# Sinkhorn attention and a bilinear feed-forward: k mixes of two head pairs together, v mixes in their own slots, and the last output tile copied by two engines

## The chip, the cores and the metric

The kernel runs on one core of a Trainium2 chip. The time is device microseconds of one execution; the metric is the median over runs. The kernel before has a median of 260.51 us of 3 runs (257.8 to 262.68).

## The reference

Four batches, eight heads, 768 positions, head size 64, and for every head an 8 x 8 matrix `sort_net`. Five rounds of exponential and row and column normalisation (Sinkhorn) turn it into P. P then mixes the eight blocks of 96 positions of k and of v, each block of q attends to its own mixed block, and the result goes through a bilinear feed-forward.

```python
for _ in range(5):
    P = np.exp(P - np.max(P, axis=-1, keepdims=True))
    P = P / (np.sum(P, axis=-1, keepdims=True) + 1e-09)
    P = P / (np.sum(P, axis=-2, keepdims=True) + 1e-09)
k_sorted = einsum('bhij,bhjcd->bhicd', P, k_blocks)     # v_sorted likewise
scores = q_block @ k_sorted_block.T / sqrt(64)          # 96 x 96 per block
attn_out = softmax(scores) @ v_sorted_block
x = attn_out with heads side by side                    # 3072 x 512
out = ((x @ w_a) * (x @ w_b)) @ w_out                   # 512 -> 1536 -> 512
```

## The kernel before, in words

Work is cut into 16 *pairs* g of two heads; pair g belongs to batch b = g // 4, and hp = g % 4. A pair's attention has these stages:

- `stage_q` (L165) transposes q on TensorE (PE) into a PSUM tile `q_ps`, and VectorE (DVE) copies it to `qT`. For pairs of batches 2 and 3, `q_by_dma` (L191) does this with one DMA transpose on SP's queue instead.
- `stage_mix` (L180) mixes k or v with P: 12 matmuls of 128 columns, each with a weight of 64 columns, so that the two heads of a pair use the left and the right half of the array. The result is a PSUM tile `mix` of two banks. `evac_k` or `evac_k_natural` (L212) copies it to `kT` on ScalarE (ACT).
- `stage_v_natural` (L196), for batches 2 and 3: two matmuls of 384 columns with full weights (L201), a DVE copy to `vn`, a store `vd` to DRAM on SP's queue (L207), and a load `vs` from there on POOL's queue (L208). For earlier batches v is mixed as k is, and `stage_v` (L239) transposes it on PE.
- `stage_scores` (L224): 8 matmuls into a PSUM tile `sc` and an exponential on ACT; once per half of the blocks.
- `stage_o` (L249): 8 matmuls of the exponentials with `vs` into `o_ps`, then a reciprocal and a product on DVE into `xp`; once per half.
- `to_xT` (L277, on PE and DVE) or `to_xT_dma` (L288, SP's queue) transposes `xp` into the feed-forward's input `xT`.

The feed-forward of a batch has 72 *steps*. 48 of them are `ffn_a` and `ffn_b` (L307, L314): four matmuls of 384 columns at L302 into a PSUM bank `pf`. After `ffn_a`, ACT copies it to `a_sb`; after `ffn_b`, DVE multiplies the two into `hT`. The last 24 steps are `ffn_out` (L328): three matmuls of 512 columns at L335 into `po`. Every fourth of these ends a tile of 128 rows, which ACT (c even) or DVE (c odd) copies to `o_sb` (L340), and two stores on SP's queue take it to `out`.

The order on PE is written by hand throughout. The order on ACT and DVE is by hand only in the parts of the program under `manual_schedule(engines=fast)`: the lead, and the block just ahead of the steps (L479 to L486). Elsewhere a scheduler orders ACT, DVE, SP and POOL by when things come ready in its own reckoning, and each of them then runs strictly in that order.

The lead (up to about 38 us in the profile) does Sinkhorn, the loads of weights, and the first halves of pairs 0 to 3. Then the loop of steps begins, and attention is hung between the steps: `after[s]` lists what follows step s. The dictionary `second` (L488) places the second halves of pairs 0 to 3: Q1 is `stage_q` for blocks 4 to 7, S1 the scores, V1 the transpose of v, O1 the product with v, X1 the transpose into `xT`. For later pairs, `C` (L451) mixes, `R` (L468) does the scores and `O` (L474) the rest. For batches 2 and 3 their slots are R at r = (b-1) 72 + 8 + 15 hp, C at r - 12 and O at r + 6.

PSUM has a pool `psA` of two tiles of two banks (mix, sc, o_ps), `psB` of one tile (q_ps, vs_ps, xt_ps) and `psF` of three banks (pf, po). The pool `ld` holds three each of k, v and q; `load_pair(g + 3)` (L81, POOL's queue) is called in `C(g)`, and its transfers wait until pair g has been read. `kT` has 5 buffers, `vs` 3.

Of the kernel before, what the change touches and what calls it, by code (L numbers as in the profile page):

```python
# [22 lines left out]
def kernel(  # L23
# [11 lines left out]
    nc = tc.nc  # L35
    P = 128
    B, H, S, D = q.shape
# [3 lines left out]
    DMODEL = H * D  # L41
# [5 lines left out]
    HP = H // 2  # L47
# [31 lines left out]
    BD = 2  # L79
# [76 lines left out]
    def copy(eng, out, in_):  # L156
        if eng is nc.scalar:
            nc.scalar.copy(out=out, in_=in_)  # L158
        else:
            eng.tensor_copy(out=out, in_=in_)  # L160

    def blocks(h):
        return (0, NB) if h is None else (h * NBH, NBH)

    def stage_q(g, pool, tag, eng, h=None):  # L165
        q2 = loaded[g][2]
        i0, n = blocks(h)
        p0, np_ = i0 * CG, n * CG
        q_ps = pool.tile([P, NCH, np_], BF16, tag=tag, name="q_ps")
        for c in range(NCH):  # L170
            for e in range(2):
                nc.tensor.matmul(q_ps[e * D:(e + 1) * D, c, :],  # L172
                                 lhsT=q2[p0:p0 + np_, e, c * D:(c + 1) * D],
                                 rhs=ident[p0:p0 + np_, p0:p0 + np_], is_transpose=True)
        if (g, "qT") not in st:
            st[g, "qT"] = qtp.tile([P, NB, NCH, CG], BF16, tag="qT", name="qT")
        copy(eng, st[g, "qT"][:, i0:i0 + n].rearrange("p i c t -> p c i t"),
             q_ps.rearrange("p c (i t) -> p c i t", i=n))

    def stage_mix(g, what, pool, tag):  # L180
        src2 = loaded[g][0 if what == "k" else 1]
        mix = pool.tile([P, 2, 512], FP32, tag=tag, name="mix")
        for c in range(NCH):
            for e in range(2):
                nc.tensor.matmul(  # L185
                    mix[e * D:(e + 1) * D, c // 4, c % 4 * P:(c % 4 + 1) * P],
                    lhsT=src2[:, e, c * D:(c + 1) * D],
                    rhs=s_all[:, 2 * g + e], start=True, stop=True)
        st[g, what] = mix

    def q_by_dma(g):  # L191
        qT = qtp.tile([P, NCH, P], BF16, tag="qT", name="qT")
        nc.sync.dma_start_transpose(out=qT, in_=loaded[g][2].rearrange("p e w -> p (e w)"))
        st[g, "qT"] = qT
# [17 lines left out]
    def evac_k_natural(g, eng):  # L212
        copy(eng, _ap(kTs[g % NKV], 0, [[S + PAD, P], [NCH, P], [1, NCH]]),
             _ap(st[g, "k"], 0, [[1024, P], [1, P], [P, NCH]]))

    def evac_k(g, eng):
        copy(eng, _ap(kTs[g % NKV], 0, [[S + PAD, P], [CG, NCH], [BLK, NB], [1, CG]]),
             _ap(st[g, "k"], 0, [[1024, P], [P, NCH], [CG, NB], [1, CG]]))

    def evac_v(g, eng, h):  # L220
        copy(eng, _ap(vTs[g % NKV], h * HK, [[2 * HK, P], [CG, NCH], [BLK, NBH], [1, CG]]),
             _ap(st[g, "v"], h * NBH * CG, [[1024, P], [P, NCH], [CG, NBH], [1, CG]]))
# [105 lines left out]
    def ffn_out(b, t, c, part, pool):  # L328
        hT = hTs[b]
        c0 = t * HW + c * P  # L330
        if part == 0:
            st[b, t, c] = pool.tile([P, DMODEL], FP32, tag="F", name="po")
        po = st[b, t, c]
        for m in range(part * KO // NPO, (part + 1) * KO // NPO):
            nc.tensor.matmul(po, lhsT=hT[:, m, c0:c0 + P], rhs=w_out_sb[:, m, :],  # L335
                             start=(m == 0), stop=(m == KO - 1))
        if part < NPO - 1:
            return
        o_sb = ffp.tile([P, DMODEL], FP32, tag="o_sb", name="o_sb", bufs=6)
        copy(nc.scalar if c % 2 == 0 else nc.vector, o_sb, po)  # L340
        for u in range(2):
            nc.sync.dma_start(
                out=_ap(out, (b * S + t * NBH * BLK + 2 * c + u) * DMODEL,
                        [[NCH * DMODEL, NBH * CG], [1, DMODEL]]),
                in_=o_sb[u * NBH * CG:(u + 1) * NBH * CG])
# [18 lines left out]
    with tc.manual_schedule(engines={mybir.EngineType.PE}):  # L364
# [68 lines left out]
        with tc.tile_pool(name="psA", bufs=2, space=PSUM) as psA, \  # L433
                tc.tile_pool(name="psB", bufs=1, space=PSUM) as psB, \
                tc.tile_pool(name="psF", bufs=3, space=PSUM) as psF:
            def Q1(g):
                stage_q(g, psB, "B", nc.vector, 1)

            def S1(g):
                stage_scores(g, psA, "A", 1)  # L440

            def V1(g):
                stage_v(g, psB, "B", 1)

            def O1(g):
                stage_o(g, psA, "A", 1)

            def X1(g):
                to_xT(g, psB, "B", 1, nc.vector)

            def C(g):  # L451
                if g >= BD * HP:
                    stage_mix(g, "k", psA, "A")
                    evac_k_natural(g, nc.scalar)
                    stage_v_natural(g, psA, "A", nc.vector)
                else:
                    stage_q(g, psB, "B", nc.vector)
                    stage_mix(g, "k", psA, "A")
                    evac_k(g, nc.scalar)
                    stage_mix(g, "v", psA, "A")  # L460
                    for h in range(2):
                        evac_v(g, nc.vector, h)
                if g + 3 < B * HP:
                    load_pair(g + 3)
                if BD * HP <= g + 1 < B * HP:
                    q_by_dma(g + 1)

            def R(g):  # L468
                stage_scores(g, psA, "A", 0)
                stage_scores(g, psA, "A", 1)  # L470
                if g < BD * HP:
                    stage_v(g, psB, "B")

            def O(g):  # L474
                stage_o(g, psA, "A", 0)
                stage_o(g, psA, "A", 1)
                to_xT_dma(g)

            with tc.manual_schedule(engines=fast):  # L479
                g = HP - 1  # L480
                parts = {}
                for n_, (m, w_sb) in enumerate(((0, w_a_sb), (0, w_b_sb), (1, w_a_sb))):
                    parts[m, w_sb is w_b_sb] = ffn_mm(0, m, 0, w_sb, psF, 0, KA - 1)
                    if n_ == 0:
                        stage_o(g, psA, "A", 0)
                to_xT(g, psB, "B", 0, nc.vector)  # L486

            second = {0: [(Q1, 0)], 1: [(Q1, 1)], 2: [(S1, 0)], 3: [(V1, 0)], 4: [(S1, 1)],  # L488
                      5: [(O1, 0), (V1, 1)], 6: [(Q1, 2)], 7: [(X1, 0)], 8: [(S1, 2), (O1, 1)],
                      9: [(V1, 2)], 10: [(Q1, 3)], 11: [(X1, 1)], 12: [(S1, 3), (O1, 2)],  # L490
                      13: [(V1, 3)], 14: [(X1, 2)], 15: [(O1, 3)], 17: [(X1, 3)]}

            NSL = 4 * KO + 2 * 3 * NPO
            after = {s: [] for s in range(-NSL, B * NSL)}
            for s, u in second.items():
                after[s] += u
            for g in range(HP, B * HP):
                b, hp = divmod(g, HP)
                if b < BD:
                    r = (b - 1) * NSL + 28 + 10 * hp  # L500
                    c_, o_ = r - 4, r + 4
                else:
                    r = (b - 1) * NSL + 8 + 15 * hp
                    c_, o_ = r - 12, r + 6
                after[c_].append((C, g))
                after[r].append((R, g))
                after[o_].append((O, g))
            s = 0
            for b in range(B):
                steps = []  # L510
                for m, t in ([(m, t) for t in range(2) for m in range(KO)] if b == 0 else
                             [(m, t) for m in range(KO) for t in range(2)]):
                    for f, u in ((ffn_a, False), (ffn_b, True)):
                        pf = parts.pop((m, u), None) if (b, t) == (0, 0) else None
                        steps.append(lambda f=f, m=m, t=t, b=b, pf=pf: f(b, m, t, psF, pf))
                for t in range(2):
                    for c in range(3):
                        for part in range(NPO):
                            steps.append(lambda t=t, c=c, part=part, b=b:
                                         ffn_out(b, t, c, part, psF))  # L520
                for step in steps:
                    step()
                    for f, g in after[s]:
                        f(g)
                    s += 1
# [29 lines left out]
```

## Time and profile before

| what | value |
|---|---|
| median of the timed runs | 260.51 us |
| the profiled execution's own time | 626.5 us |
| its span | 624.7 us |
| first pf matmul, last matmul's end | 38.54 us, 620.08 us |
| PE weight loads, busy | 249.5 us (40%) |
| chain that ended last, PE's share | 96% |
| stores of out, 48 of 128 KB | 2.3 us to land |
| vd store; vs load (192 KB), to land | 3.9 us; 3.9 to 4.0 us (medians) |

The profiled execution was far slower than the timed ones. In the page, a group is a line of code, engine, operation and tiles, with the number of instructions, busy time, mean length, and the idle time ahead of them with what ended it. In the chain of waits in order of time, each row has a start, a length, an engine, a tile and a line. In the timeline, the bracket at the end of a row gives the engine's idle time before it and what ended it.

### The profile page before, as it was taken

How to read it: one execution, taken by the hardware profiler on the slowest of the kernel's cores; microseconds unless marked ns; L12 is line 12 of the kernel's file. 1: busy time of each engine (PE TensorE's matmuls, PEld its weight loads, DVE VectorE, ACT ScalarE, POOL GpSimd, SP SyncE). 2: the span in 40 equal slices, each digit the busy share in tenths (PEclk: the TensorE clock that was granted, in tenths of full speed). 3: DMA queues.
4: the chain of work that ended last, by engine and by line, in shares of the span. 5: the costliest groups of instructions: out<-in, count | busy, mean ns of one | idle time of the engine just before them, and what ended most of it. 6: DMA issues, size and time to landing. Idle time of an engine off the chain costs nothing.

```text
span 624.7 us, 5272 instructions
## 1 busy us (share of the span) xinstructions
PE 612.4 (98%) x2140; PEld 249.5 (40%) x2153; DVE 120.7 (19%) x268; ACT 99.2 (16%) x176; POOL 62.3 (10%) x83
## 2 busy tenths in 40 slices
PE   9999999999999999999999999999999999999997
PEld 2554445544443344444333344444433334334221
DVE  4342322322211122121110122121201111111000
ACT  2322112122010121212010121212010011111000
POOL 5561001101230010101000100000000000000000
DMA  9796002314493151312122301010112100000021
GB/s 152 112 202 105 1 0 39 41 10 51 74 128 72 42 64 26 50 26 50 43 47 47 67 1 38 9 31 14 26 34 47 34 0 0 1 0 0 18 50 34
DMA packets 50776, 27.88 MB, mean 45 GB/s; under 512 B 30400, under 2 KB 47296, under 8 KB 50752
## 3 DMA queue, kind: packets, MB, share of 16 engines
q0 software_dynamic: 29712, 15.73, 19.2%
q1 hardware_dynamic: 21040, 11.81, 8.4%
q8 instruction: 17, 0.28, 0.2%
q14 instruction: 7, 0.06, 0.0%
HBM read 29.89 MB, written 7.86 MB: 60 GB/s over the span
## 4 chain that ended last, share of the span: by engine, by line
PE 96%; DMA 2%; issue 1%; POOL 1%; DVE 0%; ACT 0%
PE pf L302 55%; PE po L335 27%; PE o_ps L258 3%; PE w_ps L361 3%; PE mix L185 2%; PE sc L230 2%; DMA w_b_sb<-in_moe_w_b_dram 2%; PE q_ps L172 1%; PE mix L201 1%; PE vs_ps L244 1%; PE xt_ps L283 0%; POOL w_a_sb L143 0%; POOL w_b_sb L143 0%; POOL s_all L351 0%; ACT o_sb L158 0%
## 5 line engine op out<-in xcount | busy, mean ns | idle before, releaser
L302 PE MATMUL pf<-xT,w_a_sb 128*128 128x384 bf16 x384 | 194.0, 684 | 1.0 <-DMA w_b_sb<-in_moe_w_b_dram 0.5
L302 PE MATMUL pf<-xT,w_b_sb 128*128 128x384 bf16 x384 | 192.2, 681 | 0.0
L335 PE MATMUL po<-w_out_sb,hT 128*128 128x512 bf16 x276 | 168.5, 832 | 3.7 <-issue 3.7
L319 DVE TENSOR_TENSOR hT<-a_sb,pf 128x384 bf16<-128x384 bf16 x96 | 53.2, 555 | 270.8 <-PE pf L302 270.7
L302 PEld LDWEIGHTS <-w_a_sb 128*128 128x128 bf16 x384 | 65.6, 173 | 98.0 <-issue 96.7
L302 PEld LDWEIGHTS <-w_b_sb 128*128 128x128 bf16 x384 | 64.3, 172 | 91.5 <-issue 90.8
L335 PEld LDWEIGHTS <-hT 128*128 128x128 bf16 x288 | 49.2, 173 | 112.0 <-issue 111.8
L311 ACT CAST a_sb<-pf 128x384 bf16<-128x384 f32 x96 | 46.0, 479 | 301.5 <-PE pf L302 301.5
L158 ACT COPY o_sb<-po 128x512 f32<-128x512 f32 x16 | 9.4, 586 | 134.1 <-PE po L335 114.7
L160 DVE COPY o_sb<-po 128x512 f32<-128x512 f32 x8 | 5.5, 692 | 98.1 <-PE po L335 98.1
L264 DVE TENSOR_TENSOR xp<-o_ps,rec 96x512 bf16<-96x512 f32 x32 | 21.7, 682 | 0.7
L361 PE MATMUL w_ps<-warm_sb 128*128 128x512 bf16 x32 | 19.3, 819 | 1.7 <-DVE warm_sb L71 1.2
L262 DVE RECIPROCAL rec<-o_ps 96x8 f32<-96x8 f32 x32 | 6.4, 201 | 50.8 <-PE o_ps L258 50.8
L160 DVE CAST vn<-mix 128x768 bf16<-128x768 f32 x8 | 7.7, 957 | 16.4 <-PE mix L201 16.4
L236 ACT ACTIVATE eT_113<-sc 96x768 bf16<-96x768 f32 x12 | 9.2, 804 | 8.8 <-PE sc L230 8.7
L258 PEld LDWEIGHTS <-eT_113 96*128 96x128 bf16 x96 | 8.9, 149 | 4.3 <-issue 3.7
L258 PE MATMUL o_ps<-vs_116,eT_113 96*128 96x65 bf16 x96 | 9.3, 284 | 0.3 <-issue 0.3
L361 PEld LDWEIGHTS <-warm_sb 128*128 128x128 bf16 x33 | 4.8, 157 | 11.6 <-issue 10.3
L236 ACT ACTIVATE eT_114<-sc 96x768 bf16<-96x768 f32 x10 | 7.6, 803 | 9.6 <-PE sc L230 9.5
L351 POOL TENSOR_TENSOR s_all<-mask,p_col 128x1024 bf16<-128x1024 bf16 (+1 forms) x5 | 7.2, 1455 | 12.5 <-ACT p_col L403 12.5
L236 ACT ACTIVATE eT_115<-sc 96x768 bf16<-96x768 f32 x10 | 7.6, 803 | 3.4 <-PE sc L230 3.4
L258 PEld LDWEIGHTS <-eT_114 96*128 96x128 bf16 x80 | 6.8, 143 | 2.9 <-issue 2.9
(202 smaller groups left out, 244.7 us busy)
## 6 DMA issues: line engine op xcount, KB each, us to landing
out_dram<-o_sb SPq DMA_DIRECT2D x48, 128.0 KB, 2.3
w_a_sb<-in_moe_w_a_dram POOLq DMA_DIRECT2D x4, 384.0 KB, 7.7
w_b_sb<-in_moe_w_b_dram POOLq DMA_DIRECT2D x4, 384.0 KB, 9.0
w_out_sb<-in_moe_w_out_dram POOLq DMA_DIRECT2D x3, 512.0 KB, 8.8
vd<-vn SPq DMA_DIRECT2D x8, 192.0 KB, 3.9
q_first<-in_q_dram POOLq DMA_DIRECT2D x2, 384.0 KB, 8.1
vs_118<-vd POOLq DMA_DIRECT2D x3, 192.0 KB, 4.0
vs_116<-vd POOLq DMA_DIRECT2D x3, 192.0 KB, 3.9
```

What stands on the lines that cost most here:

```text
L158: nc.scalar.copy(out=out, in_=in_)
L160: eng.tensor_copy(out=out, in_=in_)
L185: nc.tensor.matmul(mix[e * D:(e + 1) * D, c // 4, c % 4 * P:(c % 4 + 1) * P], lhsT=src2[:, e, c * D:(c + 1) * D], rhs=s_all[:, 2 * g + e], ...
L230: nc.tensor.matmul(sc[:, e, i * BLK:(i + 1) * BLK], lhsT=kT[e * D:(e + 1) * D, blk * BLK:blk * BLK + P], rhs=(qT[e * D:(e + 1) * D, blk] i ...
L236: nc.scalar.activation(out=eT[:, h, :, 0:HB], in_=sc[0:BLK, :, 0:HB], func=AF.Exp, scale=float(scale))
L258: nc.tensor.matmul(o_ps[:, e, i * (D + 1):(i + 1) * (D + 1)], lhsT=eT[:, h, e, i * BLK:i * BLK + P], rhs=vs[:, h * NBH + i, e * (D + 1):(e ...
L264: nc.vector.tensor_tensor(out=_ap(xp, h * NBH * 2 * D, [[NB * 2 * D, BLK], [D, 2], [2 * D, NBH], [1, D]]), in0=_ap(o_ps, 1, [[1024, BLK], ...
L302: nc.tensor.matmul(pf[:, 0:HW], lhsT=w_sb[:, kc, m * P:(m + 1) * P], rhs=xTs[b][:, kc, t * HW:(t + 1) * HW], start=(kc == 0), stop=(kc == ...
L311: nc.scalar.copy(out=a_sb, in_=pf[:, 0:HW])
L319: nc.vector.tensor_tensor(out=_ap(hTs[b], m * S + t * HW, [[KO * S, P], [CG, NBH], [NBH * CG, NCH], [1, CG]]), in0=st[b, m, t].rearrange(" ...
L335: nc.tensor.matmul(po, lhsT=hT[:, m, c0:c0 + P], rhs=w_out_sb[:, m, :], start=(m == 0), stop=(m == KO - 1))
L361: nc.tensor.matmul(w_ps[:, 0:cols], lhsT=warm_sb[:, 0:P], rhs=warm_sb[:, 0:cols], start=True, stop=True)
```

## The change

- Q1 takes its PSUM tile from `psA` instead of `psB`. Q1 of pair 0 moves from behind step 0 to ahead of it, and Q1 of pair 1 from behind step 1 to behind step 0.
- For pairs of batches 2 and 3, `C` is replaced by two functions. `K2(g)`, for even hp, at the slot where `C(g)` stood, mixes k of g and of g + 1 one after the other, with their copies to `kT` on ACT. `CV(g)`, for every pair, five steps after the slot where `C(g)` stood, mixes v and then does what followed in `C`: the loads of pair g + 3 and the q transpose of pair g + 1. R and O stay where they were.
- For the very last output tile (batch 3, t = 1, c = 2), ACT copies the left 256 columns and DVE the right 256.

```diff
-        copy(nc.scalar if c % 2 == 0 else nc.vector, o_sb, po)
+        if (b, t, c) == (B - 1, 1, 2):
+            nc.scalar.copy(out=o_sb[:, 0:DMODEL // 2], in_=po[:, 0:DMODEL // 2])
+            nc.vector.tensor_copy(out=o_sb[:, DMODEL // 2:], in_=po[:, DMODEL // 2:])
+        else:
+            copy(nc.scalar if c % 2 == 0 else nc.vector, o_sb, po)
...
             def Q1(g):
-                stage_q(g, psB, "B", nc.vector, 1)
+                stage_q(g, psA, "A", nc.vector, 1)
...
             def C(g):
-                if g >= BD * HP:
-                    stage_mix(g, "k", psA, "A")
-                    evac_k_natural(g, nc.scalar)
-                    stage_v_natural(g, psA, "A", nc.vector)
-                else:
-                    stage_q(g, psB, "B", nc.vector)
-                    stage_mix(g, "k", psA, "A")
-                    evac_k(g, nc.scalar)
-                    stage_mix(g, "v", psA, "A")
-                    for h in range(2):
-                        evac_v(g, nc.vector, h)
+                stage_q(g, psB, "B", nc.vector)
+                stage_mix(g, "k", psA, "A")
+                evac_k(g, nc.scalar)
+                stage_mix(g, "v", psA, "A")
+                for h in range(2):
+                    evac_v(g, nc.vector, h)
+                more(g)
+
+            def more(g):
                 if g + 3 < B * HP:
                     load_pair(g + 3)
                 if BD * HP <= g + 1 < B * HP:
                     q_by_dma(g + 1)
+
+            def K2(g):
+                for u in (g, g + 1):
+                    stage_mix(u, "k", psA, "A")
+                    evac_k_natural(u, nc.scalar)
+
+            def CV(g):
+                stage_v_natural(g, psA, "A", nc.vector)
+                more(g)
...
                 to_xT(g, psB, "B", 0, nc.vector)
-
-            second = {0: [(Q1, 0)], 1: [(Q1, 1)], 2: [(S1, 0)], 3: [(V1, 0)], 4: [(S1, 1)],
+                Q1(0)
+
+            second = {0: [(Q1, 1)], 2: [(S1, 0)], 3: [(V1, 0)], 4: [(S1, 1)],
...
-                after[c_].append((C, g))
+                if b < BD:
+                    after[c_].append((C, g))
+                else:
+                    if hp % 2 == 0:
+                        after[c_].append((K2, g))
+                    after[c_ + 5].append((CV, g))
```

## The prediction

> **What bounds the kernel now.** I read the page's busy times first, then its costliest groups, then the chain that ended last in order of time.
>
> ```profile
> PE 612.4 (98%) x2140; PEld 249.5 (40%) x2153; DVE 120.7 (19%) x268; ACT 99.2 (16%) x176; POOL 62.3 (10%) x83
> L160 DVE CAST vn<-mix 128x768 bf16<-128x768 f32 x8 | 7.7, 957 | 16.4 <-PE mix L201 16.4
> L158 ACT COPY o_sb<-po 128x512 f32<-128x512 f32 x16 | 9.4, 586 | 134.1 <-PE po L335 114.7
> L160 DVE COPY o_sb<-po 128x512 f32<-128x512 f32 x8 | 5.5, 692 | 98.1 <-PE po L335 98.1
> ```
>
> TensorE (PE) is busy 98% of 624.7 us and the others wait for it. But this execution took 626.5 us and the timed runs 260.51. The chain gives its pace:
>
> ```profile
> 119.85 1.73 PE mix L185 x24
> ...
> 227.16 0.86 PE mix L185 x12
> 228.02 0.86 PE mix L201 x2
> 228.88 5.32 PE pf L302 x12
> 234.20 1.26 PE o_ps L258 x16
> 235.46 16.08 PE pf L302 x36
> 251.54 0.86 PE sc L230 x16
> ```
>
> 16.08 / 36 = 447 ns for a 384-column matmul, 1.16 ns per column; at that pace the 442,368 columns of the dense part alone take 515 us. The timed runs cannot have had it. So I carry PE stretches over to the timed pace, and leave durations of DVE, ACT and DMA as they are. At that pace waits appear which the trace hides, and these decide.
>
> **What the Trainium skill says.** "TensorE: Matmul & The Clock Gate", Part 1, gives N/2.4 + 2.5 ns between warm matmuls: 162.5 ns for 384 columns. The trace disagrees (447, a ratio of 2.75). As a test: the stretch from the first pf (38.54 us) to the last matmul (620.08) is 581.5; divided by 2.75 it is 211. With the lead (38.5), the tail (4.6 from there to the span's end) and 1.8 between span and execution time that makes 256. The median is 260.5, so the timed pace is about that price, with some 5 us of waits, or more if the lead is shorter too. A step (four matmuls of 384, or three of 512) is then 0.65 us. "TensorEngine Tiling (Array Packing)", Key Properties: changing the tiling mode drains TensorE. No drain is seen in the trace: 12 k mixes in 64-column tiles take 0.86, 24 in one go 1.73. The clock page, Part 2, has 398/2.4 = 166 ns of fixed latency for a lone warm matmul, my upper price of a drain. "DMA: Bandwidth & Descriptors", on the anatomy of one DMA, gives 2.0 us + bytes/436e3: 2.5 us for 192 KB. The trace has 1.8 to 4.1 and 3.8 to 4.5 for the two hops of v: it is slower, so I use the trace.
>
> **The change part by part, at the timed pace.**
>
> *Q1 in psA, Q1(0) earlier.*
>
> ```profile
> 43.68 0.36 DVE L160 COPY xT<-xt_ps 128x384 bf16<-128x384 bf16 x1 [2.17 <-PE xt_ps L283]
> 44.09 0.46 PE L302 MATMUL pf<-xT,w_a_sb 128*128 128x384 bf16 x1 [0.45 <-DVE xT L160]
> 45.16 0.36 DVE L160 COPY qT<-q_ps 128x384 bf16<-128x384 bf16 x1 [1.12 <-PE q_ps L172]
> 45.57 0.61 PE L172 MATMUL q_ps<-ident,q_first 64*64 64x64 bf16 x12
> ```
>
> PE idles 0.45 for the xT copy before step 0: Q1(0) (0.45 of PE in the trace, 0.16 scaled) now sits in that gap. DVE copies xT first, as its order is by hand there, so step 0 is not later. Before, Q1(1) waited in the one psB buffer for Q1(0)'s copy (0.36 + about 0.1 of hand-over), covered only by step 1 (one matmul, 0.16): 0.3 exposed. After, it takes the psA buffer that o_ps of pair 3 left. Gain 0.16 + 0.3 = 0.45. Q1(2) and Q1(3) stood one step (0.65) after a V1 in psB: the vs copy is 0.42, behind O1's reciprocal and product (0.20 + 0.68) at step 5. 1.3 + hand-over against 0.65 + 0.2 of PE leaves some 0.4, twice. In psA they follow a score exponential or an O1 product by two steps or more: 1.3 or more of cover for 0.8 to 0.9 of work; without it they would pay up to 0.5. I take 0.5 gained of 0 to 1.0, as DVE may be late anyway.
>
> *k mixes in pairs.* The same 8 x 12 matmuls and 8 kT copies; nothing is added. Mode changes go from 16 to 8 (into 64-column tiles and out again, per pair before, per two pairs now). 8 x 0 (the trace) to 8 x 0.17 (the price) = 0 to 1.4; I take 0.6. Against it: two kT copies of 0.8 come together on ACT (before, a kT on ACT and a vn on DVE). A-copies queue behind them: 1.6 + 0.48 = 2.1 against three psF buffers, about 1.95 of steps; 0.1 to 0.2, and O two or three steps later wants the second buffer. Four sessions, 0 to 0.3 each; I take 0.3 in all. The odd pair's k is wanted 15 steps sooner. Its load is emitted 25 steps (16 us) before, takes 3.3 to 4.3, and has its buffer free: hidden; with that cover gone it would cost up to 4 per pair.
>
> *v in its own slot, five steps later.* It moves two matmuls, the DVE copy, SP's vd store, POOL's vs load, the four loads of pair g+3 and SP's q transpose of g+1. The loads have 25 steps or more to their use, and the transpose (1.2 on SP, 2.8 to land) 22 steps to R, so both are hidden. But vs is wanted at O, now 13 steps after the v mix instead of 18:
>
> ```profile
> 198.51 0.93 PE L201 MATMUL mix<-v_1182,s_all 128*128 128x384 bf16 x2
> ...
> 199.48 0.96 DVE L160 CAST vn<-mix 128x768 bf16<-128x768 f32 x1 [2.90 <-PE mix L201]
> 199.74 0.71 POOL L93 DMA_DIRECT2D v_1656<-in_v_dram  x1 [0.17 <-issue]
> 200.47 0.36 SPq L207 DMA_DIRECT2D vd<-vn  x1
> ...
> 205.14 0.79 POOL L208 DMA_DIRECT2D vs_118<-vd  x1 [4.69 <-DMA vd<-vn]
> ```
>
> From the mix's end (199.44) to the landing (205.14 + 4.2): 9.9 us. The same sum gives 9.6 to 10.2 for pairs 8 to 12, where loads of k and v run beside vd; for 13 to 15, with no loads left, about 7.3 (vs goes out 2.4 after vd). Cover: 13 x 0.65 + R 0.86/2.75 = 8.8, and 9.4 where a session lies between (pairs 9, 13). As measured, pairs 8 to 12 lack 1.1, 0.6, 0.8, 0.8 and 1.4: 4.7 us. If k's load, which can start from the earlier session, no longer runs beside vd, the path falls towards 7.3 and nothing is lost. O waiting holds the whole in-order PE, dense matmuls included, so all of it counts. Three v mixes in four also now come two steps after an O: vn queues behind two products (0.7 each) on DVE, about 0.5 late, and SP has O's xT transpose (1.2) ahead of vd: up to 1.5 in all. So 0 to 6.2; I take 1.0 (v alone still loads beside vd, half of the lateness, mostly covered).
>
> *Last tile.* ACT's 586 for 512 columns becomes the slower half. DVE takes 555 for 384 and 692 for 512, so about 418 for 256 (ACT 372): 0.17 off the tail, the two stores (2.3) unchanged. DVE is idle there, so the cover is sure.
>
> Sum: -0.45 - 0.5 - 0.6 + 0.3 + 1.0 - 0.17 = -0.4, thus 260.5 - 0.4 = 260.1. In the profiled execution's own terms, should the slow pace recur, only 0.45 + 0.1 + 0.17 goes: 626.5 becomes 625.8, because 13 steps of 1.77 (23 us) hide any v path.
>
> **Rivals.** *(a) vs is late at every O.* Place: the first o_ps matmul. In favour: 9.6 to 10.2 against 8.8. Against: 7.3 when no load is near. With the full 6.2 and ACT's 1.2, less 0.7 of sure gains, 267.2; it passes 2% (5.2 us) from about 0.75 us per pair over eight pairs. *(b) Tile switches and psB waits are dearer than I priced them.* The 5 us or more of waits that the pace leaves could lie there. 1.4 + 1.0 + 0.45 + 0.17 gives 257.5 with vs in time; at twice that price for the switch and psB terms, 255. Against: the trace has no drain. *(c) The regrouping does nothing,* as the switches are free and the v path is covered: only Q1 and the tail count, 259.9.
>
> **How the numbers follow.** Main case 0.45 (260.1), (a) 0.2 (267 if full, 264 if partial; past 2% in 0.15), (b) 0.15 (257.5 to 255; past 2% in 0.1), (c) 0.2 (259.9). The main case's own range is 257.5 to 262.5; the shown runs alone spread from 257.8 to 262.7. With both rivals in, 255.5 to 265.5. About 2% is what a measurement of this kernel can tell from no change. Faster 0.1, same 0.75, slower 0.15.
>
> **What would show it.** Right: Q1(0) before the first full pf with no 0.45 wait on xT; 24 k mixes in one piece of the chain, v mixes apart; the last o_sb in two halves near 0.4. Rival (a): at a fast pace, PE waits before o_ps released by the DMA vs<-vd. Rival (b): a gap or a longer first matmul at each mix L185. Wrong altogether: PE waiting on mix for k loads, or psF waits behind two kT copies longer than 0.3.

## The result, and the profile after

The changed kernel takes 266.84 us (266.28 to 267.13, 4 runs) against 259.69 us for the kernel before (257.80 to 262.68, 4 runs): 1.030 times as long, with an interval of 1.023 to 1.037. The forecast was 260.1 and no measurable change; the time is that of rival (a), worked out as 267.2. Here and below, a time is the median of all executions, while a ratio, with its 95% interval, leaves out those more than 1.5% above the fastest of their kernel.

The profile of the changed kernel ran at the pace of the timed runs (span 265.3 us), which that of the kernel before had not. So the kernel before was profiled again, unchanged (run `e1_before_again`, span 258.2 us), and all comparisons below are with that trace; the trace that the prediction was read from is called the first trace. The difference of the spans, 7.1 us, is that of the medians.

First the page's busy times and the group of the vn copy, now of the changed kernel.

```profile
PE 242.5 (91%) x2139; PEld 138.4 (52%) x2153; DVE 117.3 (44%) x269; ACT 97.3 (37%) x176; POOL 62.4 (24%) x83
...
L160 DVE CAST vn<-mix 128x768 bf16<-128x768 f32 x8 | 7.6, 947 | 0.0
```

The same first line of the unchanged kernel:

```profile
PE 241.7 (94%) x2140; PEld 138.3 (54%) x2153; DVE 117.7 (46%) x268; ACT 98.0 (38%) x176; POOL 62.3 (24%) x83
```

PE has the same work (242.5 and 241.7 us) in a longer span: the loss is waiting. In the vn row, DVE no longer idles before its copy of the v mix (0.0): the mix is always there before DVE gets to it. The view of who waited for whom, of PE alone, says for what PE waits (total us, times, longest). Changed kernel:

```profile
PE pf L302 <- DMA xT<-xp: 5.9, 1, 5.9
PE o_ps L258 <- DMA vs_118<-vd: 4.1, 2, 2.8
PE o_ps L258 <- DMA vs_116<-vd: 2.0, 2, 1.8
...
PE o_ps L258 <- DMA vs_117<-vd: 1.2, 1, 1.2
PE pf L302 <- DVE xT L160: 0.7, 1, 0.7
```

Unchanged kernel:

```profile
PE pf L302 <- DMA xT<-xp: 5.8, 1, 5.8
...
PE pf L302 <- DVE xT L160: 1.2, 2, 0.7
...
PE q_ps L172 <- DVE qT L160: 0.2, 1, 0.2
```

The 7.3 us for vs<-vd are new. The 5.9 us for xT, which look like the greatest loss if one reads the trace of after alone, are in both kernels and cost nothing in the comparison. The waits on Q1's side are smaller after: 0.7 for DVE's xT copy instead of 1.2, and the 0.2 for qT is gone.

The chain of waits in order of time shows one late pair, 9. (A q behind an engine's name stands for its sequencer, which waits and issues, and "issue" is time for which the profile shows no wait.) Its v mix ends at 111.0; the rows follow its result to o_ps:

```profile
110.69 0.60 DVE xp L264
111.29 0.43 DVE vn L160
111.72 0.36 issue
112.08 0.55 DVE hT L319
112.62 5.15 DMA vd<-vn
117.80 0.04 POOLq L208
117.84 1.10 issue
118.95 3.73 DMA vs_116<-vd
122.68 0.04 issue
122.72 0.71 PE o_ps L258 x16
```

vn starts behind O's second product; vd goes out at 112.62, behind pair 8's xT transpose on SP (111.32 to 112.53); it takes 5.15 us to land beside a load of v that POOL issued at 111.30; POOL needs 1.2 until vs goes out; vs takes 3.73. That is 11.7 us where PE arrived after 9.9, and it waits 1.82. Pairs 8 to 12 wait 1.30, 1.82, 1.19, 2.80 and 0.19 us, pairs 13 to 15 not at all. In the unchanged kernel no pair waits.

The longest wait costs more than itself. These rows give, for stretches of the changed kernel's trace, busy times of PE, weight loads, DVE, ACT and POOL, then the granted clock (1.00 is TensorE's full speed), DMA share and GB/s:

```profile
146.00:149.00 3.00, 0.29 (x2) 0.01 (x1) 0.00 (x0) 0.59 (x1) 0.00 (x0) 1.00 0.93 185
149.00:151.00 2.00, 1.91 (x20) 1.10 (x21) 1.39 (x4) 0.00 (x0) 0.00 (x0) 0.67 0.26 69
151.00:153.00 2.00, 2.00 (x7) 0.66 (x5) 0.31 (x1) 0.00 (x0) 0.00 (x0) 0.50 0.21 39
153.00:155.00 2.00, 2.00 (x11) 0.92 (x10) 0.00 (x0) 0.59 (x1) 0.00 (x0) 0.98 0.30 60
```

After the 2.80 us wait for pair 11's vs the granted clock falls to 0.50 until about 153. From that O's start to the next k mix the changed kernel takes 8.12 us (149.09 to 157.21), the unchanged one 6.44 (143.75 to 150.19) for the same matmuls: 1.7 us more.

**The account of the 7.1 us**, from the starts of the same matmuls in the two traces. Lost: the late vs put the O of pairs 8 to 12 off by 7.9 us (the view's 7.3 counts each wait from the modelled end of the matmul before, which lies up to 0.17 behind the start that the next would have had); the lowered clock after the longest wait 1.7; the wait for xT 0.1; the tail 0.2 (below). Gained: Q1 1.1; the k mixes in pairs 0.9; the lead, which no edit touches, 0.1; and 0.7 that no edit aims at, because the clock is at 0.50 after the wait for xT too, for 2.7 us of PE's running in the changed kernel and 4.0 in the unchanged one. The sum is +7.1.

### The profile page after: what moved, and what is told of

It is laid out like the page before. It is cut to its first block, busy times and chain, and to the rows that moved or that the text cites. A ratio compares the mean times of both kernels' runs of the same rounds, so it can differ in the third digit from the quotient of the medians.

```text
span 265.3 us, 5280 instructions
## 1 busy us (share of the span) xinstructions
PE 242.5 (91%) x2139; PEld 138.4 (52%) x2153; DVE 117.3 (44%) x269; ACT 97.3 (37%) x176; POOL 62.4 (24%) x83
## 4 chain that ended last, share of the span: by engine, by line
PE 62%; DMA 18%; DVE 5%; issue 3%; SPq 1%; ACT 0%; POOLq 0%; DVEq 0%
PE pf L302 32%; PE po L335 20%; DMA vd<-vn 8%; DMA vs_118<-vd 3%; PE o_ps L258 3%; DMA vs_116<-vd 3%; PE mix L185 2%; DMA xT<-xp 2%; DVE xp L264 2%; PE sc L230 2%; DMA vs_117<-vd 2%; DVE hT L319 1%; DVE vn L160 1%; PE vs_ps L244 1%; PE q_ps L172 1%
## 5 line engine op out<-in xcount | busy, mean ns | idle before, releaser
L302 PE MATMUL pf<-xT,w_a_sb 128*128 128x384 bf16 x384 | 79.0, 327 | 6.8 <-DMA xT<-xp 5.9
L302 PE MATMUL pf<-xT,w_b_sb 128*128 128x384 bf16 x384 | 79.1, 328 | 0.0
L335 PE MATMUL po<-w_out_sb,hT 128*128 128x512 bf16 x275 | 64.7, 387 | 0.6 <-issue 0.2
L302 PEld LDWEIGHTS <-w_b_sb 128*128 128x128 bf16 x384 | 35.9, 98 | 29.0 <-issue 6.7
L302 PEld LDWEIGHTS <-w_a_sb 128*128 128x128 bf16 x384 | 36.9, 98 | 24.7 <-issue 1.3
L335 PEld LDWEIGHTS <-hT 128*128 128x128 bf16 x288 | 27.9, 99 | 32.7 <-issue 2.2
L365 PE MATMUL w_ps<-warm_sb 128*128 128x512 bf16 x32 | 10.1, 474 | 1.4 <-DVE warm_sb L71 1.2
L208 POOL DMA_DIRECT2D vs_116<-vd x3 | 2.4, 794 | 21.8 <-DMA vd<-vn 14.9
L208 POOL DMA_DIRECT2D vs_118<-vd x3 | 2.4, 794 | 21.5 <-DMA vd<-vn 21.5
L258 PE MATMUL o_ps<-vs_118,eT_115 96*128 96x65 bf16 x80 | 3.6, 194 | 4.1 <-DMA vs_118<-vd 4.1
L365 PEld LDWEIGHTS <-warm_sb 128*128 128x128 bf16 x33 | 3.5, 117 | 6.1 <-issue 3.3
```

The lines of the kernel that those rows point to most:

```text
L258: nc.tensor.matmul(o_ps[:, e, i * (D + 1):(i + 1) * (D + 1)], lhsT=eT[:, h, e, i * BLK:i * BLK + P], rhs=vs[:, h * NBH + i, e * (D + 1):(e ...
L302: nc.tensor.matmul(pf[:, 0:HW], lhsT=w_sb[:, kc, m * P:(m + 1) * P], rhs=xTs[b][:, kc, t * HW:(t + 1) * HW], start=(kc == 0), stop=(kc == ...
L365: nc.tensor.matmul(w_ps[:, 0:cols], lhsT=warm_sb[:, 0:P], rhs=warm_sb[:, 0:cols], start=True, stop=True)
```

## The experiments

The short theory after the result: **1**, the v path, from the v mix to the landing of vs, is longer than the 13 steps left to it. Its rivals: the k mixes in pairs cost something, or the wait for xT is new. **1a** and **1b** are about why it is long: transfers beside it, or the queues ahead of its hops. **2** is about the wait for xT that both kernels have, **3** about the tail.

**The unchanged kernel again** (`e1_before_again`).

> The kernel before, unchanged, for a profile at the pace of the timed runs. Theory 1 (late vs): no wait of PE for the DMA vs<-vd before any o_ps, and a total of PE waits about 7 us below that of the changed kernel. Rival (the wait for xT): the changed kernel's 5.9 us wait of pf for the DMA xT<-xp is new, so it is absent here or under 1 us. If it is here too with about the same length, it is no part of the loss. Time about 260 either way.

260.24 us, 1.001 times the kernel before (0.998 to 1.004). No wait for vs; the wait for xT is there with 5.8 us. The rival falls.

**Q1 and the last tile alone** (`e2_q1_and_tail`): the changed kernel with C as it was in the kernel before, in its old slots (the edit to the slots is shown).

```diff
-                if b < BD:
-                    after[c_].append((C, g))
-                else:
-                    if hp % 2 == 0:
-                        after[c_].append((K2, g))
-                    after[c_ + 5].append((CV, g))
+                after[c_].append((C, g))
```

> The changed Q1 and the split last tile alone; mixes as in the kernel before. Predicted gain 0.45 + 0.5 + 0.17 = 1.1 us: about 258.6 to 259.2. If the loss came from Q1 in psA, it would be near 266 instead.

259.74 us, 0.997 (0.995 to 1.000): at the edge of what can be told, and less than forecast. The trace says where the rest went. The first long stretch of pf (28 matmuls) begins at 42.13 us instead of 43.34, but PE then waits 6.2 us for xT instead of 5.8, loses 0.4 more to the lower clock behind that wait, and the tail is 0.2 longer. The Q1 edit does not cause the loss.

**The v mix early, pairs kept** (`e3_pairs_v_early`).

```diff
-                    after[c_ + 5].append((CV, g))
+                    after[c_ + 1].append((CV, g))
```

> The changed kernel with CV one step after the old slot of C instead of five (17 steps to O instead of 13). Theory 1 (late vs): the 7.3 us of waits for vs<-vd mostly go, as 4 steps are 2.6 us and each wait was 1 to 3: about 258 to 260. Rival (k mixes in pairs cost, by two kT copies on ACT or by loads): it stays at 265 to 267.

259.10 us, 0.997 (0.995 to 1.000). One wait for vs is left, 0.8 us, and the loss is gone with four steps of distance. Pairs of k mixes cost nothing.

**The v mix late, and nothing else** (`e4_v_late_only`): the kernel before, with k mixed pair by pair at the old slot and CV five steps later.

```diff
+            def K2(g):
+                for u in (g,):
+                    stage_mix(u, "k", psA, "A")
+                    evac_k_natural(u, nc.scalar)
...
+                    after[c_].append((K2, g))
+                    after[c_ + 5].append((CV, g))
```

> The kernel before with only the v mix five steps later; k mixes one by one at the old slots, Q1 and last tile as before. Theory 1: waits for vs<-vd as in the changed kernel or worse, as k loads stand beside vd again: 267 to 269. Rival (pairs cost): about 260.

The four executions took 267.42, 271.50, 271.80 and 272.57 us, against a median of 259.96 for the kernel before beside them; no interval was formed. The lowest alone is within the forecast. Waits of PE in the one at 271.50:

```profile
PE pf L302 <- DMA xT<-xp: 7.2, 1, 7.2
PE o_ps L258 <- DMA vs<-vd: 6.6, 3, 2.9
```

Three O wait 2.90, 0.85 and 2.86 us for vs, and after each of the two long waits the granted clock is at 0.50 for 3.4 us, which the forecast does not have. With e3 it shows that the five steps make the loss, and that they are enough to make it; its size when they stand alone is less sure (7.5 us above that median in the lowest execution, 11.7 in the median of the four).

**Loads out of the way** (`e5_loads_early`): seven buffers for k and v, so that their loads for batch 3 run before batch 2's v mixes. SP's order stays as it is.

```diff
-            to = ld.tile([P, 2, W], BF16, tag=name, name=name)
+            to = ld.tile([P, 2, W], BF16, tag=name, name=name, bufs=3 if name == "q2" else 7)
```

> The changed kernel with seven buffers for k and seven for v instead of three, so that the loads for pairs 11 to 14 run before batch 2's v mixes and not beside their vd and vs; SP's order is the same. Theory 1a (the v path is long because loads of k and v run beside vd): the waits of o_ps for vs<-vd fall from 7.3 us to under 2, and the time to about 260 to 262. Rival 1b (the path is long by its own hops, by DVE's products and SP's transposes ahead of vd): the waits stay at 5 or more, time 265 to 267.

260.61 us, 1.003 (1.000 to 1.005). The waits of PE:

```profile
PE pf L302 <- DMA xT<-xp: 3.9, 1, 3.9
PE o_ps L258 <- DMA vs<-vd: 1.7, 2, 1.1
```

With the v mix as late as in the changed kernel, 1.7 us of waits are left of 7.3, and vd lands in 2.2 us (median) instead of 3.7. 1a holds: most of the lateness is the loads in flight beside vd. The edit moved k and v together, but the traces tell which of them counts. In the changed kernel, when the vd of pairs 9 to 11 start, no k load is in flight, only a load of v and the xT transpose (and for pair 9 a load of q), and they take 5.15, 4.26 and 4.88 us. Here the same three have the transpose beside them, too (and pair 9 the load of q), but no load of v, and take 2.22, 2.10 and 2.26. So it is the load of v that makes the difference, and taking k away was not enough. Loads are not all of it: pair 12's vd takes 3.89 here with no load beside it, which stays open.

**vd off SP's queue** (`e8_vd_on_act`).

```diff
-        nc.sync.dma_start(out=vd, in_=vn.rearrange("p c e d -> p (c e d)"))
+        nc.scalar.dma_start(out=vd, in_=vn.rearrange("p c e d -> p (c e d)"))
```

> The changed kernel with the vd store issued from ACT's queue, so that it doesn't stand behind the xT transposes on SP. Theory 1a (transfers beside it): little change, waits 6 to 7 us, time 265 to 267. Rival 1b (SP's queue holds vd up): waits fall by 2 or more, time 262 to 264.

266.04 us, 1.015 (1.005 to 1.026). The four executions lie between 263.24 and 270.41, across both forecasts, so the time decides nothing. The waits for vs are 6.5 us, as 1a says. In detail both have a part. Pair 9, whose vd had stood behind the xT transpose, waits 0.32 instead of 1.82; pair 8, with nothing ahead of it in either kernel, waits 2.33 instead of 1.30. The profiled execution, at 264.43, is faster than the changed kernel's mainly because no wait for vs is followed by a lower clock (1.7 us in the changed kernel) and the wait for xT is 5.0 instead of 5.9.

**Three steps instead of five** (`e7_v_plus3`, `after[c_ + 3]`).

> The changed kernel with CV three steps after the old slot instead of five (15 steps to O). Theory 1: each late pair gains two steps, 1.3 us; the four waits of 1.30, 1.82, 1.19 and 2.80 become about 0, 0.5, 0 and 1.5: 2 us in all instead of 7.3, time about 261 to 262. Rival (vd's lateness depends on what stands around it in its slot and not on the distance): 264 to 267.

266.90 us, 1.026 (1.018 to 1.034). The waits of PE:

```profile
PE pf L302 <- DMA xT<-xp: 6.7, 1, 6.7
PE mix L201 <- DVE xp L264: 4.9, 6, 1.0
PE o_ps L258 <- DMA vs<-vd: 1.3, 2, 0.9
```

A badly chosen slot: c + 3 is also O of the pair before, so the v mix comes right behind o_ps and waits for DVE to free one of the two psA buffers, six times, up to 1.03. The waits for vs fell to 1.3, about as theory 1 has it (pair 9 waits 0.44 and pair 10, for which none was forecast, 0.88), but the time is no measure of it.

**Seven steps** (`e11_v_plus7`, `after[c_ + 7]`), a slot with no O in it.

> The changed kernel with CV seven steps after the old slot instead of five (11 steps to O): no O or R in its slot. Theory 1 (distance to O against a path of 10 to 12 us): pairs 8 to 11 each wait 1.3 us more and pair 12 about 1.3, 13 to 15 up to 0.5: waits of 13 to 15 us in all instead of 7.3, time 272 to 275. Rival (lateness set by what stands around the slot): 264 to 268.

273.82 us, 1.051 (1.043 to 1.059). The waits of PE:

```profile
PE o_ps L258 <- DMA vs<-vd: 9.9, 6, 3.3
PE pf L302 <- DMA xT<-xp: 7.3, 1, 7.3
```

The time is as forecast, the waits are not: 9.9 us, not 13 to 15. Pairs 8 to 12 wait 1.90, 1.08, 1.81, 3.26 and 1.73. Two steps further from O's products and xT transpose the path is shorter (9.5 to 10.8 us for pairs 8 to 11, against 10.2 to 11.7 in the changed kernel), which takes back part of the 1.3 us per pair. That the time comes out all the same is luck: the wait for xT is 1.4 us longer, and the clock is low for longer, at 0.50 for 20.5 us in all instead of 6.8 (10.2 about the wait for xT, 3.4 after pair 8's wait, 6.8 after the wait of 3.26).

**Pair 7's transpose on PE** (`e6_xT7_on_pe`), for the wait that both kernels have.

```diff
-                to_xT_dma(g)
+                if g != BD * HP - 1:
+                    to_xT_dma(g)
...
+                if g == BD * HP - 1:
+                    after[o_ + 4].append((lambda g: to_xT(g, psB, "B", None, nc.vector), g))
```

> The kernel before, but pair 7's transpose into xT is done on PE and DVE (8 matmuls, one copy), not on SP's queue behind q transposes that wait for loads. Theory 2 (the 5.8 us wait of pf for xT, which both kernels have, is SP's order): it goes, PE pays about 0.4 more: 254.5 to 256. Rival (the queue behind it, the vd store of pair 8, is just as late and O of pair 8 waits instead): 258 to 260.

260.07 us, 0.997 (0.993 to 1.000): the rival. The wait for xT is gone and pair 8's O waits 4.3 us for vs instead; SP's queue was late for the vd store too. So it is the queue that is late. Its rows in the unchanged kernel (start, time to issue, line, transfer):

```profile
86.82 3.32 SPq L193 DMA_TRANSPOSE qT<-q  x2
90.24 1.81 SPq L342 DMA_DIRECT2D out_dram<-o_sb  x3
92.14 1.31 SPq L290 DMA_TRANSPOSE xT<-xp  x1
```

The q transposes of pairs 10 and 11 hold SP until 90.1; the chain shows the second waiting for a q load that landed at 88.6, which had waited for a buffer that an earlier q transpose freed at 83.4. The stores of out and xT stand behind.

**Five buffers for q**, with the v mix early (`e9_q5_v_early`) and in the kernel before (`e10_before_q5`).

```diff
-            to = ld.tile([P, 2, W], BF16, tag=name, name=name)
+            to = ld.tile([P, 2, W], BF16, tag=name, name=name, bufs=5 if name == "q2" else 3)
```

> A candidate to beat both: the changed kernel with CV one step after the old slot, and five buffers for q instead of three, so that the q loads of pairs 10 and 11 do not wait for the q transposes of pairs 8 and 9 and SP's queue frees pair 7's xT transpose in time. Theory 2: the 5.7 us wait of pf for xT falls to under 1 and o_ps of pair 8 waits no more than 1: 253.5 to 256. Rival: the queue is late for its other members, as the wait has only changed its place when the transpose was taken off the queue: 258 to 260.

> The kernel before with five buffers for q and nothing else. Theory 2: the wait of pf for xT falls from 5.8 to under 1, time 254.5 to 256.5; the distance to the candidate with the same buffers is what the change's good parts bring, about 1 to 2 us. Rival: 259 to 261.

255.47 us, 0.979 (0.973 to 0.985), and 258.06 us, 0.987 (0.981 to 0.994). In the candidate the xT transpose goes out at 85.73 instead of 92.14, PE waits 2.3 for it, and no O waits for vs. In the kernel before with the same buffers the wait is still 4.3, and its time lies between the two forecasts: the transpose goes out at 87.36, 4.8 us sooner, but takes 7.73 to land instead of 4.69. Theory 2 is right that the q buffers hold the queue up, but that is only part of the wait. The first of the two is faster than both kernels; it has the change's Q1, pairs and tail as well.

**The last tile from two PSUM tiles** (`e12_two_banks`), on top of the candidate.

```diff
+                for e, p_ in enumerate((po, st["right"])):
+                    n = slice(e * DMODEL // 2, (e + 1) * DMODEL // 2)
+                    nc.tensor.matmul(p_[:, n], lhsT=hT[:, m, c0:c0 + P], rhs=w_out_sb[:, m, n],
+                                     start=(m == 0), stop=(m == KO - 1))
...
-            nc.vector.tensor_copy(out=o_sb[:, DMODEL // 2:], in_=po[:, DMODEL // 2:])
+            nc.vector.tensor_copy(out=o_sb[:, DMODEL // 2:], in_=st["right"][:, DMODEL // 2:])
```

> The candidate (v mix one step after the old slot, five q buffers), with the last tile's right half accumulated in a PSUM tile of its own (24 matmuls of 256 columns in place of 12 of 512); both halves still go to one SBUF tile. Theory 3 (the two copies of the last tile ran one after the other because they read one PSUM tile): DVE's copy now starts within 0.1 us of ACT's and the last copy ends about 0.45 us after the last matmul instead of 0.85; time as the candidate's within noise, 255. Rival (it was the shared SBUF tile): DVE's copy still starts when ACT's ends.

Timeline of the changed kernel's last copies:

```profile
260.49 0.37 ACT L341 COPY o_sb<-po 128x256 f32<-128x256 f32 x1 [4.59 <-PE po L335]
260.89 0.42 DVE L342 COPY o_sb<-po 128x256 f32<-128x256 f32 x1 [2.30 <-ACT o_sb L341]
```

and of this one:

```profile
247.96 0.37 ACT L349 COPY o_sb<-po 128x256 f32<-128x256 f32 x1 [4.51 <-PE po L340]
248.07 0.42 DVE L350 COPY o_sb<-po 128x256 f32<-128x256 f32 x1 [1.93 <-PE po L340]
```

254.19 us, 0.975 (0.969 to 0.981). Reading one PSUM tile, DVE's half is released by ACT's; with two, both are released by PE, and they overlap. The shared SBUF tile was no hindrance. Theory 3 holds: the last copy ends 0.46 us after the last matmul. What that saves, 0.4 us, is below what the times can tell. In this trace pair 10's O waits 1.7 us for vs, where in the candidate, with the same slot, none does. Pair 10's path, from the mix's end to the landing of vs, is 12.0 us in the candidate, 14.1 here and 13.2 in e3, so even the early slot only just covers it.

## Why the prediction was wrong

**The pace of a step was right**, 0.65 us (36 matmuls of 384 columns take 5.85 us in the new trace), and so was it that the first trace hid waits. That "some 5 us of waits" were left in the kernel before came out near by two errors that cancel. The lead up to the first pf takes 23.1 us in the new trace, not 38.5, and PE is busy for 222.5 us after it, not 211, as the small matmuls of attention gained less than 2.75 times (12 k mixes went from 0.86 to 0.46). PE idles 7.8 us after the first pf, 5.8 of them in the one wait for xT, which the prediction did not place.

**Q1** was right: 1.1 us by the trace for 0.95. The timeline has Q1(0) at 25.21 us, under the first xT copy, and pf's wait of 0.45 us for that copy is gone. The 0.7 us that is left of 1.2 is a later wait, which both kernels have.

**k mixes in pairs** were right, and a little under-priced: 0.9 for 0.6. Chain of the unchanged kernel, one pair:

```profile
106.86 0.46 PE mix L185 x12
107.32 0.43 PE mix L201 x2
107.75 1.95 PE pf L302 x12
109.70 0.52 PE o_ps L258 x16
```

and of the changed one, two pairs' k and one v:

```profile
180.30 0.79 PE mix L185 x24
181.09 2.06 PE pf L302 x12
183.15 0.52 PE o_ps L258 x16
183.67 1.30 PE pf L302 x8
184.97 0.33 PE mix L201 x2
```

Two pairs took 2 x (0.46 + 0.43) = 1.78. Now they take 0.79 + 2 x 0.33 and 0.11 more on the 12 pf behind the session (2.06 against 1.95): 1.56. A change into or out of 64-column tiles thus costs 0.10 to 0.13 us here (2 x 0.46 - 0.79, 0.43 - 0.33, 2.06 - 1.95). The Trainium skill, "TensorEngine Tiling (Array Packing)", Key Properties, names a drain at such a change without a price, and the first trace had shown none. ACT's two copies in a row, priced at 0.3, made no wait that the trace shows.

**The last tile** was wrong in sign: 0.17 gained was forecast, and the last copy ends 0.86 us after the last matmul (261.31 against 260.45) instead of 0.63. "The cover is sure" took two engines reading one PSUM tile to be free to do so.

**The v path** is the step that failed: "So 0 to 6.2; I take 1.0 (v alone still loads beside vd, half of the lateness, mostly covered)". Measured: 7.3. The cover was as reckoned (PE arrives 8.8 to 9.9 us after the mix's end, for 8.8 and 9.4), and the three hops were named. For the path as first measured the prediction itself had a lack of 4.7 us; taking 1.0 in its place is the greater part of the error. Two things were wrong. With k away, the path did not come down halfway: beside a load of v and with no k load in flight, the vd of pairs 9 to 11 took 4.26 to 5.15 us, no less than the 3.9 to 4.1 beside k and v in the first trace. And the products and the transpose ahead of vn and vd, which made up the upper end, do not hit alone; they hit together with the loads. Without the loads (e5, pairs 9 to 11) they leave a path of 8.2 to 8.9 us, which is covered. The path was 10.2 to 11.7 for pairs 8 to 11, against the 9.6 to 10.2 that the prediction read in the first trace, where the same work was spread over 2.4 times the time. In the unchanged kernel at the timed pace it is 16.9, 12.0, 10.0, 10.1 and 10.9 for pairs 8 to 12, behind a cover of 12.6 or more: so it was that long before the change already, which the first trace hides. Where the loads run out the path is short again, as forecast: pair 12 waits 0.19 us, pairs 13 to 15 not at all.

**What was in no case**: that a wait of 2.80 us lowers the clock for the next 3.4. Of the 9.6 us that the v mix's new place lost (7.9 and 1.7), 1.7 are of this kind. Rival (a), with every pair late by its own sum, had the mechanism, the place and, by chance, the size: it had 1.2 us for ACT's copies, which did not come, and nothing for the clock.

## What to carry to other kernels

When a step is moved closer to its consumer, its path must be summed at the top end of what neighbours can do to each hop, and not in the middle: DMA hops beside loads that the same step triggers are late together. Where a trace runs at another pace than the timed runs, a path with DMA in it can be too short there, as traffic is denser in the timed runs (here 108 GB/s on the mean against 45, and a path of 10.0 to 16.9 us against 9.6 to 10.2). A long wait found in the profile of after is evidence only once the profile of before at the same pace doesn't have it.

## What was not expected of the hardware

- PE's granted clock fell to 0.50 for some 3.4 us after an idle of 2.80 us, costing 1.7. The Trainium skill, "TensorE: Matmul & The Clock Gate", Part 1 on HAM oscillation, puts the bound at idle gaps of about 3.4 us; in these runs shorter ones were enough, 2.80 here, 2.31 in e9 and 1.90 in e11, each with 3.4 us at 0.50 behind it. But 2.33 in e8 and 2.57 in e12 left the clock at 1.00, as 1.30 and 1.82 did here, so the length of an idle time alone does not decide it. Every low stretch behind a wait lasts 3.4 us or two or three times that.
- Between vd's landing and the start of the POOL instruction that loads vs lie 0.6 us as a rule and 1.2 for pair 9, in the unchanged kernel as in the changed one; in the chain this time is "issue".
- A 192 KB store that lands in 1.8 us alone takes 3.4 to 5.2 us beside loads. The price worked out in the prediction, 2.5, fits neither; the formula behind it was for DMAs that GpSimd issues, while SP issues this store.
